# A fused attention and MLP block on one core: attention in units of two head pairs from the third query block on, with TensorE's order written out

## The chip, the core and the metric

The kernel runs on one core of a Trainium2 chip. The engines are TensorE (PE in the rows; PEld is its weight load), VectorE (DVE), ScalarE (ACT), GpSimd (POOL) and SyncE (SP), which issues the DMAs. Each works through its own queue in order, and semaphores hold an instruction until what it needs is there. The metric is the time of one execution on the device in microseconds (us), as a median over runs.

## The reference

Three stages follow each other on 2 batches of 768 tokens:

```python
# 1. attention, 8 heads of 64, a causal window of 96 keys and 8 global keys, a bias by distance
scores = scale * q @ k.T - slope[h] * dist          # only where keep
a = softmax(scores); x = a @ v                      # x: 2 x 768 x 512
# 2. channel mix
xn = (x - mean) / sqrt(var + 1e-6) * g_ln
x = x + relu(xn @ w_ch1) @ w_ch2                    # 512 -> 2048 -> 512
# 3. token mix
theta = x @ w_theta; zr, zi = x * cos(theta), x * sin(theta)
u = x + w_tok_r @ zr + w_tok_i @ zi
out = u + relu(u @ w_ch)
```

## The kernel before

**Attention** runs over 12 blocks of 128 queries (2 batches of 6). SEQ is their order, and CHUNKS groups them in twos: `[[0, 6], [1, 2], [3, 4], [5, 7], [8, 9], [10, 11]]`. The first two blocks (0 and 6, the first of each batch) see 128 keys, all others 256. A block has four head pairs p. For each pair:
- `scores` (L190): two f32 matmuls s, one for each head, on the two halves of TensorE's rows. DVE adds the bias and takes the minimum of the negated scores ("maxima", tile e, accumulator nm), ACT takes exp in place.
- `flip_probs` (L220), called flip below: TensorE transposes e into the PSUM bank pt, ACT or DVE copies it to pts.
- `values` (L235): f32 matmuls of pts with the block's v (vc) and its window's v (vw) into xa.

Per block, `finish_x` (L251) copies xa to xs on ACT, transposes it back on TensorE (xp), and DVE scales it into x2. `layer_norm` (L269) gives xn; six of the twelve blocks take two POOL operations for it (LN_DVE = 6), the others one of DVE. `make_xt` (L356) transposes xn (xnp) and splits it into xth + xtl, since a matmul in f32 precision is made of three in float32r: high x high, high x low, low x high.

**The channel mix** goes in items (c, f): chunk c of 256 tokens, f one of 16 slices of 128 hidden channels. `mlp_h` (L367) runs 12 matmuls hp, then ACT's hh (Relu) and DVE's hl; `mlp_o` (L389) runs 6 matmuls op, three for each of the chunk's two blocks, accumulated in PSUM over a group of f and then added to x2 by DVE (`add_mix`, L386). A round is 24 items: all six chunks with four f. The weights come as 58 pieces of 512 KB (raw, three buffers), each decoded to f32 by one ACT operation and three of DVE (pieces 0 to 15), and split into high and low parts by `split_w` (L338).

**The order.** A framework schedules the instructions of each engine by its own estimate and fixes one order for each. `attention` (L744) is a generator whose step n issues the scores of pair n, the flip of pair n - 2, the values of pair n - 3, and finish_x, layer_norm and make_xt at lags 6, 7 and 8. The main loop (L809) calls `steps_to` so that a chunk's xt is issued before its first item. In the first round the four f are taken in two groups of two (`beside`, L805), so that items start after two decoded pairs of pieces. TensorE's order in the attention part is thus the scheduler's: an item's matmuls are put between those of pairs one or two at a time.

`spin` (L71) issues dummy matmuls that keep TensorE busy while it would wait. PSUM has eight banks: h 2, o 2, s 2, pt 1, m 1 (L66); xp of the later blocks uses pt too.

Of the kernel before, what the change touches and what calls it, by code (L numbers as in the profile page):

```python
# [29 lines left out]
EDGE = 248  # L30
PAD = 32
# [3 lines left out]
def kernel(ctx, tc, q, kwin, v, n_pair, g_ln, wall, out):  # L35
# [12 lines left out]
    HALF = GROUP // 2  # L48
    GROUPS = [range(0, HALF), range(HALF, GROUP), *(range(f, f + GROUP) for f in range(GROUP, NF, GROUP))]
# [70 lines left out]
    maxima = []  # L120

    def behind_maximum(n):
        return tc.issue_after(maxima[n]) if n is not None else ExitStack()

# [65 lines left out]
    def scores(b, i, p, startup):  # L190
        nk = WIN if i else P
        b0 = 0 if i else WIN
        if p == 0:
            stat[b, i] = (
                at.tile([P, H], F32, tag="nm", name=f"nm{b}_{i}", bufs=2),
                at.tile([P, H], F32, tag="sm", name=f"sm{b}_{i}", bufs=2),
            )
        nm, sm = stat[b, i]
        qb, kb = qt[b, i], kt[b, i]
        s = [ps("h" if startup and p % 2 else "s", [P, nk], f"s{b}_{i}_{p}_{j}") for j in range(2)]  # L200
        k0 = WIN - nk
        for j in range(2):
            rows = slice(j * D, (j + 1) * D)
            nc.tensor.matmul(s[j], qb[rows, p, :], kb[rows, p, k0:WIN], start=True, stop=True)  # L204
        if startup:
            spin("o", f"spin{b}_{p}", 2)
        e = at.tile([P, 2, nk], F32, tag="p", name=f"e{b}_{i}_{p}", bufs=3)
# [7 lines left out]
        for j in range(2):  # L215
            h = 2 * p + j
            nc.scalar.activation(e[:, j, :], e[:, j, :], AF.Exp, bias=nm[:, h:h + 1], scale=-1.0, accum_out=sm[:, h:h + 1])  # L217
        e_t[b, i, p] = e

    def flip_probs(b, i, p, startup):  # L220
# [7 lines left out]
        pts = at.tile([P, 2, nb, P], F32, tag="pt", name=f"pts{b}_{i}_{p}", bufs=2)  # L228
        if p % 3:
            nc.scalar.activation(pts, pt, AF.Copy)  # L230
        else:
            nc.vector.tensor_copy(pts, pt)
        pts_t[b, i, p] = pts

    def values(b, i, p):  # L235
# [31 lines left out]
    LN_DVE = 6  # L267

    def layer_norm(t, at=at, gbc=gbc):  # L269
# [7 lines left out]
        if SEQ.index(t) < LN_DVE:  # L277
# [61 lines left out]
    def split_w(f):  # L339
        decode_to(2 * f + 2)  # L340
        r = []
        for d, nm in enumerate(("w1", "w2")):
# [6 lines left out]
        split_t[f] = r  # L349
# [5 lines left out]
    def make_xt(t):  # L355
# [6 lines left out]
        transposed(xn_t.pop(t), hi[:, :, sl], lo[:, :, sl], "m", f"xnp{t}")  # L362
# [3 lines left out]
    def mlp_h(c, f, tag):  # L366
# [377 lines left out]
    def attention():  # L744

        N = NTT * NPAIR

        def block(n):
            return blocks[n // NPAIR]

        def startup(n):
            return n // NPAIR < len(CHUNKS[0])

        for n in range(N + 20):
            t, p = divmod(n, NPAIR)
            if n < N:
                if p == 0:
                    loads_to(t + 2)
                scores(*blocks[t], p, startup(n))
            if 0 <= n - 2 < N:  # L760
                flip_probs(*block(n - 2), (n - 2) % NPAIR, startup(n - 2))
            if 0 <= n - 3 < N:
                values(*block(n - 3), (n - 3) % NPAIR)
            for lag, fn in ((6, finish_x), (7, layer_norm), (8, make_xt)):
                k_ = n - lag
                if k_ % NPAIR == 0 and 0 <= k_ < N:
                    tt = SEQ[k_ // NPAIR]
                    if fn is finish_x:
                        finish_x(*divmod(tt, NQ), startup(k_))
                    else:  # L770
                        fn(tt)
            yield

# [9 lines left out]
    st = attention()  # L783

    def steps_to(n):
        while n_step[0] < n:
            next(st, None)
            n_step[0] += 1

    def done_at(c):  # L790
        return NPAIR * (SEQ.index(CHUNKS[c][-1]) + 1) + 7

    spin("m", "spin", 12)
    steps_to(2)
# [10 lines left out]
    beside = [(0, 0), (0, 1), (1, 0)] + [x for c in range(2, NCH) for x in ((0, c), (1, c - 1))] + [(1, NCH - 1)]  # L805
    rest = [(g, c) for g in range(2, len(GROUPS)) for c in range(NCH)]
    work = [(g, c, f) for g, c in beside + rest for f in GROUPS[g]]
# [120 lines left out]
```

## Time and profile before

| | us |
|---|---|
| median of 3 runs | 569.44 |
| lowest, highest | 568.22, 569.63 |
| the profiled execution | 569.5 |
| its span, first to last instruction | 567.6 |
| busy: TensorE, DVE, ACT, POOL | 554.1, 366.5, 282.4, 121.8 |
| mean granted TensorE clock, share of full speed | 0.997 |

TensorE's matmuls are pipelined and a record lasts longer than the distance to the next start, so its busy time says little; the distances between starts say what a matmul costs. Records of one kind that follow each other are merged into one row of the timeline (x4 is four records).

### The profile page before, as it was taken

To read this page: it belongs to the slowest core of one execution; us is meant where nothing else is said; L and a number is where in the kernel's file an instruction comes from. 1 tells how busy PE (TensorE), PEld (TensorE's weight loads), DVE (VectorE), ACT (ScalarE), POOL (GpSimd) and SP (SyncE) were. 2 spreads that over 40 slices of the span, in tenths; PEclk is the share of its full clock that TensorE was granted. 3 is DMA by queue.
4 is the path that set the end of the run, shared out by engine and by line. 5 is a ranking of instruction groups with operands and counts; after the bars stand their busy time and mean duration, and the time that the engine had idled before them with its cause. 6 is when DMAs were issued, how large, how long until landed. Compare 5 with 4: busy or idle time off the path is not lost.

```text
span 567.6 us, 9282 instructions
## 1 busy us (share of the span) xinstructions
PE 554.1 (98%) x3532; PEld 461.9 (81%) x3532; DVE 366.5 (65%) x789; ACT 282.4 (50%) x647; POOL 121.8 (21%) x103
## 2 busy tenths in 40 slices
PE   8899999999999999999999999999999999999996
PEld 4466677777798899999999888889888888888895
DVE  6899989757458732278784524463699888871542
ACT  5887764645226511166662415561587777740110
POOL 1455420000012000030300202231033347730000
PEclk9999999999999999999999999999999999999998
DMA  8965655500003410025452000000243200000122
GB/s 271 324 214 177 218 191 205 167 1 2 0 1 112 152 34 1 1 84 208 156 186 74 1 1 1 1 2 0 75 147 120 106 1 1 1 1 1 76 74 80
DMA packets 18548, 49.18 MB, mean 87 GB/s; under 512 B 2240, under 2 KB 4288, under 8 KB 18496
## 3 DMA queue, kind: packets, MB, share of 16 engines
q1 hardware_dynamic: 18496, 48.51, 24.7%
q8 instruction: 30, 0.49, 0.4%
q14 instruction: 22, 0.18, 0.1%
HBM read 45.35 MB, written 3.15 MB: 85 GB/s over the span
## 4 chain that ended last, share of the span: by engine, by line
PE 64%; ACT 1%; DVE 1%; issue 0%; DVEq 0%; ACTq 0%
PE op L398 17%; PE acc L551 17%; PE hp L375 17%; PE thm L486 6%; PE ch L597 6%; PE xp L290 1%; ACT wt L320 0%; ACT xth L291 0%; DVE hl L380 0%; DVE w2l L347 0%; DVE x2all L387 0%; ACT w L320 0%; ACT k L494 0%; ACT k L493 0%; ACT s L499 0%
## 5 line engine op out<-in xcount | busy, mean ns | idle before, releaser
L375 PE MATMUL hp<-xth,w1h 128*128 128x256 f32 x384 | 109.0, 284 | 0.0
L375 PE MATMUL hp<-xth,w1l 128*128 128x256 f32 x384 | 108.7, 283 | 0.0
L375 PE MATMUL hp<-xtl,w1h 128*128 128x256 f32 x384 | 108.4, 282 | 0.0
L380 DVE SCALAR_TENSOR_TENSOR hl<-hp,hh 128x256 fp32r<-128x256 f32 x96 | 40.2, 420 | 79.7 <-ACT hh L379 79.4
L379 ACT ACTIVATE hh<-hp 128x256 fp32r<-128x256 f32 x96 | 36.0, 376 | 95.9 <-PE hp L375 95.9
L551 PE MATMUL acc<-tokh,z 128*128 128x512 f32 (+1 forms) x320 | 79.2, 336 | 0.0
L398 PE MATMUL op<-w2h,hh 128*128 128x512 f32 x192 | 76.9, 401 | 0.7 <-ACT hh L379 0.5
L375 PEld LDWEIGHTS hp<-xth,w1h 128*128 128x128 f32 x384 | 72.6, 189 | 6.2 <-issue 1.5
L375 PEld LDWEIGHTS hp<-xtl,w1h 128*128 128x128 f32 x384 | 72.6, 189 | 5.9 <-issue 1.7
L398 PE MATMUL op<-w2l,hh 128*128 128x512 f32 x192 | 76.1, 397 | 0.0
L398 PE MATMUL op<-w2h,hl 128*128 128x512 f32 x192 | 76.0, 396 | 0.0
L375 PEld LDWEIGHTS hp<-xth,w1l 128*128 128x128 f32 x384 | 72.6, 189 | 1.7 <-issue 1.5
L551 PEld LDWEIGHTS acc<-tokh,z 128*128 128x128 f32 x320 | 55.4, 190 | 6.5
L217 ACT ACTIVATE e<-e,nm 128x256 f32<-128x256 f32 (+1 forms) x96 | 46.2, 482 | 26.8 <-DVE nm L210 24.8
L551 PE MATMUL acc<-tokl,z 128*128 128x512 f32 (+1 forms) x160 | 53.8, 336 | 0.0
L347 POOL TENSOR_TENSOR w1l<-w,w1h 128x512 fp32r<-128x512 f32 x16 | 22.3, 1391 | 136.1 <-ACT w1h L346 136.1
L387 DVE SCALAR_TENSOR_TENSOR x2all<-op,rsall,x2all 128x512 f32<-128x512 f32 x60 | 42.8, 743 | 6.8 <-PE op L398 6.8
L513 POOL TENSOR_TENSOR x2all<-xth,xtl 128x512 f32<-128x512 f32 x12 | 18.3, 1524 | 121.2 <-DVE k L505 121.2
L398 PEld LDWEIGHTS op<-w2h,hl 128*128 128x128 f32 x192 | 36.1, 188 | 8.9 <-DVE hl L380 0.2
L210 DVE CUSTOM_DVE_ANT_0 e<-s,bias 128x256 f32<-128x256 f32 (+1 forms) x96 | 35.4, 392 | 11.4 <-PE s L204 10.6
L398 PEld LDWEIGHTS op<-w2h,hh 128*128 128x128 f32 x192 | 36.4, 190 | 5.7 <-ACT hh L379 0.7
L463 DVE TENSOR_TENSOR tokl<-wt,tokh 128x512 fp32r<-128x512 f32 x36 | 33.9, 950 | 10.3 <-ACT tokh L462 10.1
(155 smaller groups left out, 1074.1 us busy)
## 6 DMA issues: line engine op xcount, KB each, us to landing
raw<-in_wall SPq DMA_DIRECT2D x58, 512.0 KB, 3.2
k<-in_kwin SPq DMA_DIRECT2D x10, 512.0 KB, 5.7
q<-in_q SPq DMA_DIRECT2D x12, 256.0 KB, 4.0
vc<-in_v SPq DMA_DIRECT2D x12, 256.0 KB, 3.2
out<-o SPq DMA_DIRECT2D x8, 256.0 KB, 2.0
vw<-in_v SPq DMA_DIRECT2D x10, 192.0 KB, 2.7
out<-o SPq DMA_DIRECT2D x8, 128.0 KB, 2.2
vw<-in_v SPq DMA_DIRECT2D x10, 64.0 KB, 3.7
```

The lines of the kernel that those rows point to most:

```text
L210: r = nc.vector.tensor_tensor_reduce(out=e[:, j, :], in0=s[j], in1=bias[h][:, b0:b0 + nk], scale=-SCALE, scalar=3.0e38, op0=ALU.add, op1=A ...
L217: nc.scalar.activation(e[:, j, :], e[:, j, :], AF.Exp, bias=nm[:, h:h + 1], scale=-1.0, accum_out=sm[:, h:h + 1])
L347: (nc.vector if d and f >= GROUP else nc.gpsimd).tensor_tensor(lo, s, hi.bitcast(F32), ALU.subtract)
L375: nc.tensor.matmul(hp, l, r[:, kk, :], start=(n == 0), stop=(n == 3 * KD - 1))
L379: nc.scalar.activation(hh, hp, AF.Relu)
L380: nc.vector.scalar_tensor_tensor(hl, hp, 0.0, hh.bitcast(F32), ALU.max, ALU.subtract)
L387: nc.vector.scalar_tensor_tensor(x2[t], o, rsall[:, t:t + 1], x2[t], ALU.mult, ALU.add)
L398: nc.tensor.matmul(op_t[c][j], l, r, start=(f == fs[0] and n == 0), stop=(f == fs[-1] and n == 2))
L463: nc.vector.tensor_tensor(lo, src, hi.bitcast(F32), ALU.subtract)
L486: nc.tensor.matmul(mp, l[:, kk, :], r[:, kk, :], start=(n == 0), stop=(n == 3 * KD - 1))
L551: mm = nc.tensor.matmul(o, l[:, dsl], r[:, sl], start=first and not (paired and d % 2), stop=end and not (paired and d % 2 == 0))
L597: nc.tensor.matmul(mp, l[:, kk, es], r, start=(kk == 0 and m == 0), stop=(kk == KD - 1 and m == 2))
```

## The change

The first two blocks keep their order, left to the scheduler (`head_step`). From the third block on a loop over k issues, on TensorE alone in exactly the order of the code (`tc.manual_schedule`), one unit (two head pairs of a block: scores, later two flips and two values) and one item of the first round. hp of an item is cut in two halves of six matmuls with a flip between them, op in two halves by block, xp and xnp go between those. In steps 0 to 5 one piece each is decoded and split (pieces 2 to 7) and from step 7 on one piece per two steps (decoded only). The first three steps have no mix and fill up with five dummy matmuls at a time. The first round takes its four f in one group, so 48 adds replace 60. In the first two blocks' flips and in all others, ACT copies pairs 0 and 2 and DVE 1 and 3 (before: ACT 1 and 2). xs is copied right behind a block's values (`lift_x`); xnp moves from bank m to a bank h; xn is DVE's for all blocks (LN_DVE = 0); e gets a fourth buffer; a unit's scores of one head side share one bank.

```diff
-    GROUPS = [range(0, HALF), range(HALF, GROUP), *(range(f, f + GROUP) for f in range(GROUP, NF, GROUP))]
+    GROUPS = [range(f, f + GROUP) for f in range(0, NF, GROUP)]
...
+    def scores(b, i, ps_, startup):
...
+        n = len(ps_)
+        s = [ps("h" if startup and ps_[0] % 2 else "s", [P, n, nk], f"s{b}_{i}_{ps_[0]}_{j}") for j in range(2)]
+        k0 = WIN - nk
+        for a, p in enumerate(ps_):
+            for j in range(2):
+                rows = slice(j * D, (j + 1) * D)
+                nc.tensor.matmul(s[j][:, a, :], qb[rows, p, :], kb[rows, p, k0:WIN], start=True, stop=True)
...
-        if p % 3:
+        if p % 2 == 0:
             nc.scalar.activation(pts, pt, AF.Copy)
...
-    LN_DVE = 6
+    LN_DVE = 0
...
-        transposed(xn_t.pop(t), hi[:, :, sl], lo[:, :, sl], "m", f"xnp{t}")
+        transposed(xn_t.pop(t), hi[:, :, sl], lo[:, :, sl], "h", f"xnp{t}")
...
+    U = 2
+    NU = (NTT - HEAD) * U
+    LEAD = 3
+    items = [(c, f) for c in range(NCH) for f in GROUPS[0]]
...
+    with tc.manual_schedule(engines=ENGINES):
+        for k in range(LEAD + len(items) + 1):
+            j = k - LEAD
+            u = k - 1
+            mix = 0 <= j < len(items)
+            xp_of = HEAD + (k - 3) // U if k % U == 1 and 0 <= (k - 3) // U < NTT - HEAD else None
+            xt_of = HEAD + (k - 4) // U if k % U == 0 and 0 <= (k - 4) // U < NTT - HEAD else None
...
+            if 0 <= u < NU:
+                flip_probs(*unit(u)[:2], unit(u)[2][0], False)
+            if k < NU:
+                b, i, ps_ = unit(k)
+                if k % U == 0:
+                    loads_to(HEAD + k // U + 2)
+                scores(b, i, ps_, False)
...
+            if mix:
+                mlp_h(*items[j], "h", 0)
+            elif 0 < k < LEAD:
+                spin("o", f"idle{k}", 5)
+            if 0 <= u < NU:
+                flip_probs(*unit(u)[:2], unit(u)[2][1], False)
+            if mix:
+                mlp_h(*items[j], "h", 1)
+            if xt_of is not None:
+                make_xt(SEQ[xt_of])
+            if 0 <= j - 1 < len(items):
+                down(j - 1, [0])
+            if xp_of is not None:
+                finish_x(*blocks[xp_of], False)
+            if 0 <= j - 1 < len(items):
+                down(j - 1, [1])
+            if 0 < k < LEAD:
+                spin("o", f"wait{k}", 5)
+            if 0 <= u < NU:
+                for p in unit(u)[2]:
+                    values(*unit(u)[:2], p)
+                if u % U == U - 1:
+                    lift_x(*unit(u)[:2])
+            if xp_of is not None:
+                layer_norm(SEQ[xp_of])
+            if 0 <= k < 2 * GROUP - 2:
+                with behind_exp(len(maxima) - 1):
+                    split_w((k + 2) // 2, ((k + 2) % 2,))
+            elif k >= 7:
+                with behind_maximum(min(len(maxima) - 1, 16 + 4 * k + 3)):
+                    decode_to(2 * GROUP + min(NW, (k - 5) // 2))
```

Where TensorE stood in block 0_4 and 0_5 (batch 0, blocks 4 and 5; the second number of a pair's tile is p), the order before was this:

```order
L204 MATMUL s0_5_0_0_983<-k0_5_645,q0_5_644 128x256
L204 MATMUL s0_5_0_1_984<-k0_5_645,q0_5_644 128x256
L375 MATMUL hp1_0_1180<-xth1_675,w1h0_269 128x256
L227 MATMUL pt0_4_2_992<-ident_65,e0_4_2_826 128x128 x4
L246 MATMUL xa0_4_958<-pts0_4_1_956,vw0_4_500 64x128
L246 MATMUL xa0_4_958<-pts0_4_1_956,vc0_4_498 64x128
L246 MATMUL xa0_4_958<-pts0_4_1_956,vw0_4_500 64x128
L246 MATMUL xa0_4_958<-pts0_4_1_956,vc0_4_498 64x128
L204 MATMUL s0_5_1_0_1012<-k0_5_645,q0_5_644 128x256
L204 MATMUL s0_5_1_1_1013<-k0_5_645,q0_5_644 128x256
L375 MATMUL hp1_0_1180<-xtl1_676,w1h0_269 128x256
```

and now, at the end of step 9 and the beginning of step 10 (hp of item 6 stands ahead of these rows, hp of item 7 behind), it is:

```order
L429 MATMUL op1_0_1_1133<-w2h1_540,hh1_1_1120 128x512
L429 MATMUL op1_0_1_1133<-w2l1_541,hh1_1_1120 128x512
L429 MATMUL op1_0_1_1133<-w2h1_540,hl1_1_1121 128x512
L284 MATMUL xp4_1203<-ident_65,xs0_4_1149 128x128 x4
L429 MATMUL op1_0_2_1134<-w2h1_540,hh1_1_1120 128x512
L429 MATMUL op1_0_2_1134<-w2l1_541,hh1_1_1120 128x512
L429 MATMUL op1_0_2_1134<-w2h1_540,hl1_1_1121 128x512
L264 MATMUL xa0_5_1212<-pts0_5_0_1156,vw0_5_723 64x128 x2
L264 MATMUL xa0_5_1212<-pts0_5_0_1156,vc0_5_721 64x128 x2
L264 MATMUL xa0_5_1212<-pts0_5_1_1186,vw0_5_723 64x128 x2
L264 MATMUL xa0_5_1212<-pts0_5_1_1186,vc0_5_721 64x128 x2
L245 MATMUL pt0_5_2_1237<-ident_65,e0_5_2_1164 128x128 x4
```

One hp stood between a pair's scores and the next flip, and each pair's values stood alone; now op and xp stand together, and two pairs' values behind each other. Behind the last row come the four matmuls of scores of the next unit and six hp.

On DVE the same step is, from the decode of piece 9 on (the maxima of the unit stand ahead of it):

```order
L351 TENSOR_SCALAR dec9_1233<-w9_1229 128x512
L250 COPY pts0_5_1_1186<-pt0_5_1_1181 128x512
L352 SCALAR_TENSOR_TENSOR dec9_1233<-w9_1229,dec9_1233 128x512
L410 SCALAR_TENSOR_TENSOR hl1_2_1195<-hp1_2_1174,hh1_2_1194 128x256
L285 TENSOR_TENSOR x2all_70<-xp4_1203,sm0_4_914 128x512
L353 SCALAR_TENSOR_TENSOR w9_1229<-raw9_796,dec9_1233 128x512
L297 BN_STATS bn4_1221<-x2all_70 128x6
L280 TENSOR_SCALAR sm0_5_1083<-sm0_5_1083 128x8
L298 BN_AGGR mv4_1222<-bn4_1221 128x2
L281 RECIPROCAL sm0_5_1083<-sm0_5_1083 128x8
L304 SCALAR_TENSOR_TENSOR xn4_1225<-x2all_70,mv4_1222,gbc_95 128x512
```

where the program before had, around its decode of piece 9:

```order
L328 TENSOR_SCALAR dec9_2160<-w9_2156 128x512
L210 ISA e0_5_2_1036,nm0_5_981<-s0_5_2_0_1032,bias4_102 128x256
L210 ISA nm0_5_981 128x1
L210 ISA e0_5_2_1036,nm0_5_981<-s0_5_2_1_1033,bias5_103 128x256
L210 ISA nm0_5_981 128x1
L329 SCALAR_TENSOR_TENSOR dec9_2160<-w9_2156,dec9_2160 128x512
L232 COPY pts0_5_0_1046<-pt0_5_0_1041 128x512
```

Now four maxima stand together ahead of the decode, the pts copy behind its first operation, and xn (before POOL's for this block) is DVE's.

In the beginning, behind the first two blocks, TensorE now has (steps 0 and 1; idle0 are dummy matmuls, s0_1_0 and pt0_1_0 belong to the third block):

```order
L231 MATMUL s0_1_0_0_422<-k0_1_163,q0_1_162 128x256
L231 MATMUL s0_1_0_1_423<-k0_1_163,q0_1_162 128x256
L231 MATMUL s0_1_0_0_422<-k0_1_163,q0_1_162 128x256
L231 MATMUL s0_1_0_1_423<-k0_1_163,q0_1_162 128x256
L264 MATMUL xa1_0_372<-pts1_0_2_396,vc1_0_147 64x128 x2
L264 MATMUL xa1_0_372<-pts1_0_3_403,vc1_0_147 64x128 x2
L245 MATMUL pt0_1_0_456<-ident_65,e0_1_0_428 128x128 x4
L231 MATMUL s0_1_2_0_463<-k0_1_163,q0_1_162 128x256
L231 MATMUL s0_1_2_1_464<-k0_1_163,q0_1_162 128x256
L231 MATMUL s0_1_2_0_463<-k0_1_163,q0_1_162 128x256
L231 MATMUL s0_1_2_1_464<-k0_1_163,q0_1_162 128x256
```

The scores of the second unit stand behind the first flip of the first, so behind its exp; before, the scheduler had put scores of three pairs ahead of the third block's first flip.

## Rows read from the trace of the kernel before

**Rows 1.** Windows: PE, PEld, DVE, ACT, POOL busy (instructions), clock, DMA share, GB/s.

```profile
16.00:61.00 45.00, 41.44 (x310) 26.93 (x312) 42.34 (x128) 36.44 (x111) 23.46 (x19) 1.00 0.68 232
61.00:149.00 88.00, 85.68 (x648) 63.45 (x647) 69.67 (x207) 47.83 (x141) 11.51 (x12) 1.00 0.34 115
```

**Rows 2.** The chain that ended last, by time: start us, us, what.

```profile
189.28 1.64 PE op L398 x6
...
193.79 1.40 PE op L398 x6
195.19 1.42 PE hp L375 x12
```

**Rows 3.** Groups of TensorE, 60.81 to 149.11 us: records, busy us, mean ns, idle before.

```profile
L204 PE MATMUL s<-k,q 64*128 64x256 f32 x96 | 17.2, 428 | 0.0
...
L375 PE MATMUL hp<-xth,w1h 128*128 128x256 f32 x48 | 14.1, 294 | 0.0
...
L398 PE MATMUL op<-w2h,hl 128*128 128x512 f32 x25 | 10.0, 398 | 0.0
...
L290 PE MATMUL xnp<-ident,xn 128*128 128x128 f32 x24 | 3.9, 284 | 1.6 <-ACT xs L256 1.6
```

**Rows 4.** TensorE's waits, 61 to 149 us: total us, times, longest.

```profile
PE xnp L290 <- ACT xs L256: 1.6, 3, 0.8
```

**Rows 5.** TensorE's timeline from 61.45 us: start us, us, records.

```profile
61.45 0.66 PE L227 MATMUL pt<-ident,e 128*128 128x128 f32 x4
62.03 0.45 PE L246 MATMUL xa<-pts,vw 128*64 128x128 f32 x4
...
62.63 0.70 PE L204 MATMUL s<-k,q 64*128 64x256 f32 x4
63.26 0.39 PE L375 MATMUL hp<-xth,w1h 128*128 128x256 f32 x1
63.70 0.65 PE L227 MATMUL pt<-ident,e 128*128 128x128 f32 x4
```

**Rows 6.** TensorE's timeline in the first two blocks, scores of 128 keys.

```profile
5.67 0.49 PE L204 MATMUL s<-k,q 64*128 64x128 f32 x4
6.10 0.61 PE L75 MATMUL spin<-zero 128*128 128x512 bf16 x2
...
12.46 0.71 PE L204 MATMUL s<-k,q 64*128 64x128 f32 x8
13.11 0.44 PE L227 MATMUL pt<-ident,e 128*128 128x128 f32 x2
```

**Rows 7.** TensorE's timeline from 58.17 us: transposes, half an hp, op.

```profile
58.17 0.60 PE L261 MATMUL xp<-ident,xs 128*128 128x128 f32 x4
58.52 0.36 PE L375 MATMUL hp<-xth,w1h 128*128 128x256 f32 x1
...
59.32 0.40 PE L398 MATMUL op<-w2h,hh 128*128 128x512 f32 x1
```

**Rows 8.** TensorE's timeline from 30.27 us: two pairs' values in a row.

```profile
30.27 0.45 PE L246 MATMUL xa<-pts,vw 128*64 128x128 f32 x4
...
31.35 1.35 PE L204 MATMUL s<-k,q 64*128 64x256 f32 x4
```

**Rows 9.** DVE's timeline: the last operation on piece 3.

```profile
35.86 0.68 DVE L330 SCALAR_TENSOR_TENSOR w<-raw,dec 128x512 int32<-128x512 int32 x1
```

**Rows 10.** Groups by shape, 0 to 189 us: exp, maxima, add, pts, xn.

```profile
L217 ACT ACTIVATE e<-e,nm 128x256 f32<-128x256 f32 x80 | 39.9, 500 | 20.8 <-DVE nm L210 18.8 <-DVE mv L275 1.8
L210 DVE CUSTOM_DVE_ANT_0 e<-s,bias 128x256 f32<-128x256 f32 x80 | 31.4, 413 | 9.4 <-PE s L204 9.3
...
L387 DVE SCALAR_TENSOR_TENSOR x2all<-op,rsall,x2all 128x512 f32<-128x512 f32 x23 | 16.5, 743 | 3.3 <-PE op L398 3.3
...
L232 DVE COPY pts<-pt 128x512 f32<-128x512 f32 x20 | 13.7, 686 | 2.7 <-PE pt L227 2.3
...
L281 DVE SCALAR_TENSOR_TENSOR xn<-x2all,mv,gbc 128x512 f32<-128x512 f32 x6 | 4.5, 747 | 0.1
```

More of the change, by code (lines that the diff above doesn't have):

```diff
@@ L188, with soften @@
     n_step = [0]
-    def scores(b, i, p, startup):
-        nk = WIN if i else P
+    def soften(b, i, p, e, s):
+        nk = e.shape[-1]
         b0 = 0 if i else WIN
[L193 to L197, printed above, removed]
-        nm, sm = stat[b, i]
[L199 to L207, printed above, removed]
+        nm, sm = stat[b, i]
         for j in range(2):
@@ L742, in loads_to @@
             nloaded[0] += 1
[L744 to L772, printed above, removed]
     words = keep.tile([P, 2, 2], I32, name="words")
@@ L782, with behind, head_step @@
     loads_to(1)
[L783 to L791, printed above, removed]
+    HEAD = len(CHUNKS[0])
+    ROWS = range(NPAIR)
+    def behind(n):
+        return divmod(n, NPAIR)
+    def head_step(n):
+        t, p = divmod(n, NPAIR)
+        if t < HEAD:
+            if p == 0:
+                loads_to(t + 2)
+            scores(*blocks[t], [p], True)
+        for lag, fn in ((2, lambda b, i, p: flip_probs(b, i, p, True)), (3, values)):
+            if 0 <= n - lag < HEAD * NPAIR:
+                t, p = divmod(n - lag, NPAIR)
+                fn(*blocks[t], p)
+                if lag == 3 and p == NPAIR - 1:
+                    lift_x(*blocks[t])
+                    finish_x(*blocks[t], True)
     spin("m", "spin", 12)
-    steps_to(2)
+    for n in range(2):
+        head_step(n)
     next(bias_steps)
@@ L806, with unit, down @@
-    rest = [(g, c) for g in range(2, len(GROUPS)) for c in range(NCH)]
-    work = [(g, c, f) for g, c in beside + rest for f in GROUPS[g]]
-    early, done = iter(()), [0]
+    U = 2
+    NU = (NTT - HEAD) * U
+    LEAD = 3
+    items = [(c, f) for c in range(NCH) for f in GROUPS[0]]
+    def unit(k):
+        t, h_ = divmod(k, U)
+        return (*blocks[HEAD + t], [2 * h_, 2 * h_ + 1])
+    def down(j, js):
+        c, f = items[j]
+        mlp_o(c, f, GROUPS[0], js)
+        if js[-1] and c == NCH - 1 and f + GROUP < NF:
+            split_w(f + GROUP)
@@ L809 @@
+    work = [(g, c, f) for g in range(len(GROUPS)) for c in range(NCH) for f in GROUPS[g]]
+    early, done = iter(()), [ROUND]
     for n, (g, c, f) in enumerate(work):
+        if n < ROUND:
+            continue
         rnd = n // ROUND
         if n == ROUND:
-            steps_to(NTT * NPAIR + 20)
             at_es.close()
```

116 lines of the change are left out of this document (81 added, 35 removed).

## The prediction

> **What bounds the kernel now.** I read the windows first, to see which engine is full where. From 16 to 61 us DVE is busy 42.34 of 45 us; from 61 to 149 us TensorE is busy 85.68 of 88 [rows 1]. [...] The chain that ended last is TensorE's from 189.28 us on: op and hp of the channel mix, one behind the other, at 1.40 and 1.42 us, 2.82 an item [rows 2]. So what the attention part saves before that point comes off the end, if nothing new is late at the border. What stays after it (72 items, then the token mix) is not touched.
>
> A busy TensorE is not a TensorE at its peak, so I counted what it gets done. Between 60.81 and 149.11 us, 88.30 us, it runs 96 score records, 96 transposes of probabilities, 192 value records, 144 records of hp, 73 of op, 24 of xnp and 24 of xp [rows 3] (four of these groups stand there; hp and op have three forms each). An f32 matmul leaves two records, a transpose one. That is 24 head pairs, 12 items (12 hp, 6 op each) and six blocks' xp and xnp: 12 steps of the changed program, at 88.30 / 12 = **7.36 us a step**. Little of it is waiting: the longest of TensorE's waits in 61 to 149 us, xnp's, sum to 1.6 us [rows 4].
>
> The rest is the price of changing over. The timeline shows it in start times [rows 5]: four transposes 61.45 to 62.03 = 0.58, a pair's values 62.03 to 62.63 = 0.59, a pair's scores 62.63 to 63.26 = 0.63, and then a single hp 63.26 to 63.70 = 0.44. In a stream of its own kind that hp costs 1.42 / 12 = 0.118. An item takes 2.82 when it runs whole, and before 149 us it seldom does.
>
> **The change on TensorE, step by step.** The new order is flip, two pairs' scores, six hp, flip, six hp, three op, three op, two pairs' values, with xnp (even steps) or xp (odd steps) among them.
> - Flip after values: 0.58 [rows 5].
> - Two pairs' scores. No row has them with 256 keys. With 128 keys one pair takes 5.67 to 6.10 = 0.42 and two in a row 12.46 to 13.11 = 0.65 [rows 6]: the second adds 0.23. With 256 keys it adds at least that and at most a pair's whole 0.63. I take 0.43, between the two, since a record streams twice the columns while the start and the drain are paid once: **1.06**.
> - Six hp: 6 x 0.118 = 0.71. Four transposes inside a stream cost 0.355 (58.17 to 58.52), and six hp after them 0.80 instead of 0.71 (58.52 to 59.32) [rows 7]. So flip 0.355, hp 0.80, xnp or xp 0.355.
> - Six op: 1.40, and by the same rows 0.09 behind a transpose, and 0.10 for the change to values: 1.59.
> - Two pairs' values: the trace has them once, 30.27 to 31.35 = 1.08 [rows 8], against 2 x 0.59.
>
> Sum: 0.58 + 1.06 + 0.71 + 0.355 + 0.80 + 0.355 + 1.59 + 1.08 = **6.53 us**, 0.83 less than 7.36.
>
> [...]
>
> **The beginning.** The first two blocks run much as before. Steps k = 0, 1, 2 have no mix, and DVE sets their pace: it decodes pieces 0 to 3 around them (three operations each), and each unit's maxima stand behind those. The old DVE ended piece 3 at 36.5 [rows 9]. By the order, DVE has until the end of unit 2's maxima two maxima (0.41) and two pts copies (0.69) less to do than the old one until then, and two xn (0.75) more, which were POOL's [rows 10]: 36.5 - 2.2 + 1.5 = 35.8 at the same pace. Behind it stand the pts copy of unit 1, 0.69, and its values on TensorE, 1.08, so step 3, the first with a mix, starts at 37.6. I take **38**. Bounds: 35, if DVE loses the 2.7 us that it was idle in 16 to 61 us [rows 1]; 44, if in each of the three steps it waits 2 us for scores behind flips that wait for exp. The 25 new dummy matmuls (two last 0.61 [rows 6], so five some 1.4) lie under these waits; without that cover they cost 7.
>
> **The sum.** Step 3 has no op: 5.1. Steps 4 to 19: 16 x 6.53 = 104.5. Step 20 has no scores: 5.4. Step 21 is an item and xp: 3.3; step 22 an item and xnp: 3.3, plus 0.4, since x2, bn and xn (three times 0.7 on DVE) stand between xp and that xnp. Steps 23 to 26: 4 x 2.82 = 11.3. Step 27: 1.4. End of the 24 items: 38 + 5.1 + 104.5 + 5.4 + 3.3 + 3.7 + 11.3 + 1.4 = 172.7. The old program starts the op of item 24 at 189.28 with the hp of items 24 and 25 behind it, so its 24 items end at 189.28 - 2 x 1.42 = 186.4. The gain is 13.7. I take 1 us off for two places where a queue may hold: ACT's first operations on pieces 8 and 9 stand before a pts copy in step 6, and SP issues piece 9 behind loads that wait for a block's values. So 12.7. The profiled execution took 569.5 (span 567.6, 1.9 around it), the median is 569.44: 569.5 - 12.7 = **557**.
>
> **What costs nothing, and its cover.** DVE in two steady steps: 8 maxima x 0.413, ten operations of 128x512 (two pts, three of a decode, x2, xtl, bn, xn, and one add on average) at some 0.70, two hl and the small ones at some 1.6 together: 11.9 us by the means of [rows 10], less in truth, as one record begins before the last ends. Two steps of TensorE are 13.06. So xn of six blocks moved to DVE (6 x 0.75) is hidden, and the 12 adds removed (one accumulation over four f instead of two over two; 12 x 0.74 = 8.9) bring nothing by themselves; were a step shorter than 5.9, both would count in full. Inside an odd step, DVE can begin its four maxima 1.4 us after the start (the first pair's scores are out) and ends them, one decode operation and the pts copy some 2.4 later, at 3.8; xp wants that bank at 4.3. In the step that also has two adds DVE runs 1.5 us into the next; that one's maxima then end at 3.6, the four exp (0.50 each) by 6.0, and their flip comes at 6.5. Both margins are half a microsecond.
>
> **The rivals.**
> 1. *The written order waits on DVE in each step* (slower). What stands behind a late xp or flip on TensorE, the rest of the item, waits with it, and the margins are thin. xnp waits already now, up to 0.8 [rows 4]. Should every step from 3 to 19 wait 1.2 us, the time is 557 + 20 = 577. It decides from 0.9 a step on (15 us over 17 steps). Against it: 11.9 of 13.06 on DVE, and ACT busy 47.83 of 88 us [rows 1].
> 2. *Scores in twos save nothing*: 17 steps x 0.2 = 3.4 more, 560. [...]
> 3. *The beginning eats it*: step 3 at 50 instead of 38 gives 569, no change. For it speaks that scores of two pairs now wait for the maxima of the two before; against it, that DVE is full there in both programs with as much to do.
> 4. *More than forecast*: a second pair at 0.23 (-3.4) and the beginning at 35 (-3) give 550.
>
> **Chances.** Forecast 0.70 (551 to 566); rival 2 0.08; rival 4 0.08; rival 1 0.08; rival 3 0.03, and 0.03 for a gain of which only 2 to 3 us are left. 0.3% (1.7 us) is about what a measurement of this kernel can tell: faster 0.89, same 0.03, slower 0.08. The bounds (beginning -3 to +6, scores -3.4 to +3.4, waits up to +8) don't fall together; 551 to 566 holds eight in ten.
>
> **What would show it.** Right: a step of 6.4 to 6.7 us, from one first flip to the next, in 65 to 140 us, eight score records lasting 1.0 to 1.1 to the next start, the first op at about 47 us instead of 59.32, DVE idle for a tenth or more there, and the chain TensorE's alone from about 175. [...]

## The result, and the profile after

The changed kernel takes 563.26 us (median of 4 runs, 562.99 to 563.6), the kernel before 568.89 us beside it: a ratio of 0.990, 95% interval 0.988 to 0.992. It is faster by 5.6 us, or 1%; 12.7 us were forecast. The time lies inside the stated range of 551 to 566 us, but the gain is less than half of the forecast one. The profiled span is 561.4 us, 6.2 less than before.

Three windows of the changed kernel, the columns as in [rows 1]: the beginning, the steady steps, and what follows the last scores.

```profile
16.00:40.00 24.00, 19.76 (x146) 11.82 (x145) 20.12 (x58) 16.94 (x53) 6.58 (x6) 1.00 0.70 243
60.00:150.00 90.00, 90.00 (x736) 72.33 (x735) 68.49 (x221) 53.16 (x161) 5.11 (x8) 1.00 0.32 107
150.00:180.00 30.00, 27.43 (x186) 22.62 (x186) 20.54 (x39) 13.64 (x27) 6.97 (x6) 1.00 0.22 73
```

From 60 to 150 us the trace lists no wait of TensorE any more; before 60 and behind 150 it lists some. One steady step in TensorE's timeline, from a unit's first flip to the next unit's:

```profile
65.81 0.66 PE L245 MATMUL pt<-ident,e 128*128 128x128 f32 x4
66.40 1.14 PE L231 MATMUL s<-k,q 64*128 64x256 f32 x8
67.46 0.39 PE L403 MATMUL hp<-xth,w1h 128*128 128x256 f32 x1
...
68.27 0.60 PE L245 MATMUL pt<-ident,e 128*128 128x128 f32 x4
68.63 0.36 PE L403 MATMUL hp<-xth,w1h 128*128 128x256 f32 x1
...
69.42 0.40 PE L429 MATMUL op<-w2h,hh 128*128 128x512 f32 x1
...
71.34 0.44 PE L264 MATMUL xa<-pts,vw 128*64 128x128 f32 x4
...
72.37 0.44 PE L245 MATMUL pt<-ident,e 128*128 128x128 f32 x2
```

72.37 - 65.81 = 6.56 us, against 7.36 before; scores of two pairs 67.46 - 66.40 = 1.06. The middle of the forecast holds. What doesn't hold is the two ends, as the starts of the steps show. A step starts at its first flip, and from step 21 on, where there are no flips, at its first hp:

| part | forecast, us | measured, us | late by |
|---|---|---|---|
| step 3 starts | 38 | 39.89 | 1.9 |
| step 3 | 5.1 | 46.03 - 39.89 = 6.14 | 1.0 |
| steps 4 to 19 | 104.5 | 151.17 - 46.03 = 105.14 | 0.6 |
| step 20 | 5.4 | 157.68 - 151.17 = 6.51 | 1.1 |
| steps 21, 22 | 7.0 | 164.94 - 157.68 = 7.26 | 0.3 |
| steps 23 to 27 | 12.7 | 179.98 - 164.94 = 15.04 | 2.3 |

Together that is 179.98 - 172.7 = 7.3 us: the 24 items end at 179.98 instead of 172.7, which is still 6.4 earlier than the old 186.4. Nearly all of it reaches the end (6.2 us of the span).

TensorE's waits in the changed kernel, 16 to 45 us (total us, times, longest):

```profile
PE xa L264 <- DVE pts L250: 1.5, 2, 1.1
PE pt L245 <- ACT e L212: 1.4, 2, 0.8
PE pt L245 <- ACT pts L248: 1.2, 1, 1.2
```

Step 3 has two short ones, for DVE's copy of the probabilities and for DVE's x2:

```profile
43.95 0.66 PE L284 MATMUL xp<-ident,xs 128*128 128x128 f32 x4 [0.28 <-DVE pts L250]
...
46.03 0.63 PE L245 MATMUL pt<-ident,e 128*128 128x128 f32 x4 [0.40 <-DVE x2all L285]
```

The waits from 145 to 190 us:

```profile
PE op L429 <- DVE hl L410: 1.4, 2, 1.1
PE xnp L313 <- DVE rsall L305: 0.7, 1, 0.7
PE xnp L313 <- DVE xn L304: 0.4, 1, 0.4
```

The waits for xnp are in steps 20 and 22. The waits for hl are at the border, that is in the last items of the first round, steps 23 to 27. ACT, DVE, POOL and TensorE there:

```profile
172.62 0.62 ACT L370 ACTIVATE w2h<-w 128x512 fp32r<-128x512 f32 x1
173.14 0.66 ACT L347 ACTIVATE dec<-raw 128x512 int32<-128x512 uint32 x1
173.71 0.62 ACT L370 ACTIVATE w1h<-w 128x512 fp32r<-128x512 f32 x1
173.88 0.69 DVE L348 SCALAR_TENSOR_TENSOR dec<-w,dec 128x512 int32<-128x512 int32 x1
174.23 0.36 ACT L409 ACTIVATE hh<-hp 128x256 fp32r<-128x256 f32 x1
174.45 1.29 POOL L371 TENSOR_TENSOR w1l<-w,w1h 128x512 fp32r<-128x512 f32 x1 [2.43 <-ACT w1h L370]
...
174.66 1.63 DVE L349 SCALAR_TENSOR_TENSOR w<-raw,dec 128x512 int32<-128x512 int32 x1
...
176.22 0.41 DVE L410 SCALAR_TENSOR_TENSOR hl<-hp,hh 128x256 fp32r<-128x256 f32 x1
...
176.68 0.50 PE L429 MATMUL op<-w2h,hl 128*128 128x512 f32 x1 [1.08 <-DVE hl L410]
```

The hp of the item whose hh and hl stand in these rows had ended at some 172.2. Its hh comes 2 us later, behind a decode and two splits in ACT's queue. Its hl starts 1.6 us after hh has ended, behind a decode operation in DVE's queue that takes 1.63 us instead of 0.69. The chain that ended last runs through that operation and DVE's next ones until 178.95, and not through TensorE:

```profile
174.66 1.63 DVE w L349
176.29 0.34 DVE hl L410
...
178.95 1.20 PE op L429 x4
```

In the beginning DVE is idle for 3.9 of 24 us. Its timeline there:

```profile
20.11 1.45 DVE L352 SCALAR_TENSOR_TENSOR dec<-w,dec 128x512 int32<-128x512 int32 x1
...
23.43 1.09 DVE L280 TENSOR_SCALAR sm<-sm 128x8 f32<-128x8 f32 x1
...
28.38 0.43 DVE L351 TENSOR_SCALAR dec<-w 128x512 int32<-128x512 int32 x1 [1.69 <-ACT w L343]
...
35.61 0.68 DVE L353 SCALAR_TENSOR_TENSOR w<-raw,dec 128x512 int32<-128x512 int32 x1
...
37.90 0.69 DVE L250 COPY pts<-pt 128x512 f32<-128x512 f32 x1
```

The last decode ahead of step 3, the maxima behind it and this pts copy come 1.8 us after the forecast 35.8 for the maxima's end (37.59). Ahead of that DVE waits 1.69 us for ACT's first operation on piece 2, and two of its operations take longer, 1.45 instead of 0.69 us (the second of piece 1's decode) and 1.09 instead of 0.17 (sm).

### The profile page after: what moved, and what is told of

It is laid out like the page before. It is cut to its first block, busy times and chain, and to the rows that moved or that the text cites. A ratio compares the mean times of both kernels' runs of the same rounds, so it can differ in the third digit from the quotient of the medians.

```text
span 561.4 us, 9278 instructions
## 1 busy us (share of the span) xinstructions
PE 546.8 (97%) x3554; PEld 461.9 (82%) x3557; DVE 359.8 (64%) x783; ACT 280.6 (50%) x647; POOL 103.4 (18%) x91
## 4 chain that ended last, share of the span: by engine, by line
PE 66%; ACT 1%; DVE 1%; issue 0%; DVEq 0%; ACTq 0%
PE op L429 18%; PE hp L403 18%; PE acc L582 17%; PE thm L517 6%; PE ch L628 6%; PE xp L313 1%; DVE w L349 0%; ACT wt L343 0%; DVE hl L410 0%; ACT xth L314 0%; DVE dec L348 0%; ACT k L525 0%; ACT k L524 0%; ACT s L530 0%; ACT y L523 0%
## 5 line engine op out<-in xcount | busy, mean ns | idle before, releaser
L403 PE MATMUL hp<-xth,w1h 128*128 128x256 f32 x384 | 111.3, 290 | 0.0
L429 PE MATMUL op<-w2h,hh 128*128 128x512 f32 x192 | 78.5, 409 | 0.0
L409 ACT ACTIVATE hh<-hp 128x256 fp32r<-128x256 f32 x96 | 35.8, 374 | 74.4 <-PE hp L403 74.4
L205 DVE CUSTOM_DVE_ANT_0 e<-s,bias 128x256 f32<-128x256 f32 (+1 forms) x96 | 33.5, 397 | 16.8 <-PE s L231 16.7
L429 PEld LDWEIGHTS op<-w2l,hh 128*128 128x128 f32 x192 | 36.2, 188 | 3.8
```

Of the source, the lines that this page charges most:

```text
L205: r = nc.vector.tensor_tensor_reduce(out=e[:, j, :], in0=s[j], in1=bias[h][:, b0:b0 + nk], scale=-SCALE, scalar=3.0e38, op0=ALU.add, op1=A ...
L409: nc.scalar.activation(hh, hp, AF.Relu)
L429: nc.tensor.matmul(op_t[c][j], l, r, start=(f == fs[0] and n == 0), stop=(f == fs[-1] and n == 2))
```

## The experiments

**The changed kernel again**, as a base on one chip for the second group of runs.

> The changed kernel itself, unedited, so that the kernels beside it are compared with it on one chip: the ratio of 0.990 to the kernel before is expected again, and steps 23 to 27 at 15.0 us. It also says how far one profile of the same kernel differs from another in the start of step 3 (39.9 before).

0.9903 (0.9887 to 0.9919), 563.91 us; step 3 starts at 40.36, steps 23 to 27 take 15.03. So a start can differ by 0.5 between two profiles of one kernel, a step's length by 0.05. Most of the 0.5 lies ahead of the first scores, which start at 6.06 and at 6.42: counted from there, step 3 starts after 33.83 and 33.94 us. Where the ratios below are weighed, this run is the base.

**Decode held at the border.**

```diff
+        relus.append((r.ins, r2.ins))
...
-        decode_to(2 * GROUP * (rnd + 1) + min(NW, n % ROUND // 2))
+        with tc.issue_after(relus[ROUND - 1][0]), tc.issue_after(relus[ROUND - 1][1]):
+            decode_to(2 * GROUP * (rnd + 1) + min(NW, n % ROUND // 2))
```

> Pieces 16 and up are decoded only behind the relu operations of the 24th item on ACT and DVE; nothing else is moved. Theory A (at the border the decode of pieces 16 to 18, two operations of 0.67 us on ACT and two of 0.69 us on DVE each, stands ahead of hh and hl of items 22 and 23): steps 23 to 27 shrink from 15.05 us to about 13.0, the 24 items end near 178.0 instead of 179.98, and the time falls by about 2 us, to 561.3. [...] Theory C (the decode is then late in the second round): the border shrinks, but the total does not.

0.9855 (0.9835 to 0.9876), 561.84 us. The timeline of ACT, DVE and POOL with the decode held:

```profile
175.22 0.63 ACT L370 ACTIVATE w1h<-w 128x512 fp32r<-128x512 f32 x1 [0.67 <-PE hp L404]
175.76 0.36 ACT L410 ACTIVATE hh<-hp 128x256 fp32r<-128x256 f32 x1
175.99 1.30 POOL L371 TENSOR_TENSOR w1l<-w,w1h 128x512 fp32r<-128x512 f32 x1 [1.52 <-ACT w1h L370]
176.03 0.67 ACT L343 ACTIVATE w<-raw 128x512 f32<-128x512 f32 x1
176.16 0.42 DVE L411 SCALAR_TENSOR_TENSOR hl<-hp,hh 128x256 fp32r<-128x256 f32 x1 [0.88 <-ACT hh L410]
```

The splits are there as before, but hh now stands ahead of the decode, hl follows it at once, and TensorE waits for neither: steps 23 to 27 take 177.95 - 165.11 = 12.84 us, near the 12.7 of the forecast. That is theory A. The ratio falls by as much and more (0.9903 to 0.9855, some 2.7 us), so nothing is seen to be paid back later.

**xnp behind half of op in steps 20 and 22.**

```diff
-            if xt_of is not None:
+            if xt_of is not None and k < NU:
                 make_xt(SEQ[xt_of])
             if 0 <= j - 1 < len(items):
                 down(j - 1, [0])
+            if xt_of is not None and k >= NU:
+                make_xt(SEQ[xt_of])
```

> In steps 20 and 22, which have no scores, xnp stands behind the first half of op instead of ahead of it. Theory A (xnp waits there for xn and rsall, 1.0 and 0.66 us, because a step without scores is shorter than DVE's way from xp over x2, bn and xn): step 20 shrinks from 6.51 to about 5.6 us, step 22 from 3.88 to 3.4 to 3.9, and the time falls by 1.0 to 1.4 us, to 562. Theory B (the wait only moves, to hp of the item that reads the block, or DVE's queue is late for all that follows): steps 20 to 22 together keep their 13.8 us and the time stays within 0.4 us of 563.3.

0.9893 (0.9875 to 0.9911), not to be told from the base. Step 20 takes 5.82 instead of 6.51 us, step 22 3.42 instead of 3.88, but the twelve hp behind it last 2.14 instead of 1.57: they wait for that block's xth and xtl. Up to the end of these hp 0.6 us are saved. It is theory A for step 20 and theory B for step 22.

**Both at the border**: the hold, and the later xnp in step 20 alone.

```diff
+            if xt_of is not None and k == NU:
+                make_xt(SEQ[xt_of])
```

> Two edits at the border together: pieces 16 and up are held behind the relu operations of the 24th item (as in the first of these runs, which took some 2.3 us off), and in step 20 alone xnp stands behind the first half of op (step 22 as in the changed kernel, since its wait only moved). Theory A (the two losses lie one behind the other on TensorE and add up): steps 20 to 22 take 13.1 instead of 13.8 us, steps 23 to 27 12.7, and the time is 3.0 us under the changed kernel, 560.5 to 561, a ratio of 0.985. Theory B (the later xnp makes ACT and DVE late at the border again): no more than the 2.3 us of the hold alone.

0.9835 (0.9807 to 0.9862), 561.7 us, the fastest of the kernels that leave nothing out. Steps 20 to 22 take 164.54 - 151.49 = 13.05 us, steps 23 to 27 12.84. By the steps this is theory A: 0.7 + 2.2 of the lost 7.3 us are explained and got back. By the time alone it can't be told from the hold alone (0.9855).

**No dummies.**

```diff
-                spin("o", "idle0", 5)
...
-            elif 0 < k < LEAD:
-                spin("o", f"idle{k}", 5)
...
-            if 0 < k < LEAD:
-                spin("o", f"wait{k}", 5)
```

> The 25 dummy matmuls of steps 0 to 2 are left out. Theory A (they lie under waits, as forecast): step 3 starts at 39.9 less the one stretch that has no wait behind it, idle0 at 22.6 to 23.8, so between 38.8 and 39.9, and the time is 562.2 to 563.3. [...] Theory C (they cost what they last): step 3 starts 3 us earlier or more, and the time is 560 or less.

0.9914 (0.9894 to 0.9934), 565.02 us; step 3 starts at 40.50 and lasts 7.01. Windows of this kernel, the columns as in [rows 1]:

```profile
24.00:28.00 4.00, 2.08 (x18) 1.17 (x14) 2.65 (x12) 3.06 (x10) 0.97 (x2) 1.00 0.71 254
28.00:32.00 4.00, 2.23 (x22) 1.71 (x20) 3.81 (x13) 3.65 (x12) 0.75 (x1) 1.00 0.66 213
32.00:36.00 4.00, 2.95 (x16) 2.21 (x18) 3.98 (x10) 1.31 (x4) 1.06 (x2) 0.60 0.29 115
36.00:40.00 4.00, 4.00 (x24) 2.74 (x24) 2.27 (x10) 2.91 (x10) 1.67 (x2) 0.55 0.36 131
```

In this profile TensorE is busy for 4.31 of the 8 us from 24 to 32, then the granted clock is 0.60 and 0.55 in 32 to 40 us (1.00 in the changed kernel), and the scores of unit 2 take 2.01 instead of 1.16 us. The waits for pts, 1.5 us in all with the dummies, are 4.0 without. But the time shows no loss from it: the ratio can't be told from the base's 0.9903, and the start of step 3, counted from the first scores, is 34.52, 0.6 to 0.7 later. The earlier starts of theories A and C did not come. So the dummies cost nothing that these runs show, and what they save is not shown to reach the time.

**Scores of unit 0 early.**

```diff
             if k == 0:
+                loads_to(HEAD + 2)
+                scores(*unit(0), False)
                 flip_probs(*blocks[1], 2, True)
...
-            if k < NU:
+            if 0 < k < NU:
```

> In the beginning the scores of unit 0 (two pairs of the third block) stand ahead of the last flips and values of the second block, instead of behind them and the dummies. Theory A (in 16 to 40 us DVE idles for 3.9 us because its maxima of unit 0 come only at 25.3, after TensorE's written order let the scores run at 23.8): the maxima begin at 20 to 22, step 3 starts at 37.5 to 38.5 instead of 39.9, step 3 no longer waits for pts, and the time falls by 1.5 to 2.5 us, to 561 to 562. Theory B (DVE has that much to do in any order): step 3 starts at 39.4 or later and the time stays within 0.5 us of 563.3.

0.9882 (0.9863 to 0.9902), not to be told from the base. The first pair's scores run at 15.4, the second's at 17.1, but step 3 starts at 39.61: 0.3 and 0.75 earlier than in the two profiles of the changed kernel, or some 0.4 counted from the first scores (33.48). Step 3 takes 5.78 instead of 6.13. That is less than half of theory A.

**Decode not held in steps 0 to 5.**

```diff
-                with behind_exp(len(maxima) - 1):
-                    split_w((k + 2) // 2, ((k + 2) % 2,))
+                split_w((k + 2) // 2, ((k + 2) % 2,))
```

> In steps 0 to 5 the six pieces that are decoded and split there are no longer held behind the maxima and exp of the newest unit; the scheduler puts them where it finds room. Theory A (DVE idles at 26.6 to 28.4 us because the first operation of piece 2 on ACT is held behind the exp of unit 0, and this is half of the 1.9 us by which step 3 starts late): that idle stretch is filled, step 3 starts at 38.0 to 39.0 and the time falls by 1 to 2 us. Theory B (decoding ahead only puts the same work ahead of the maxima and exp for which the flips wait): step 3 starts at 39.9 or later, TensorE's waits for e and pts before 45 us grow above 5 us, and the time is the same or up to 2 us more.

0.9976 (0.9962 to 0.9991), 567.4 us. TensorE's waits, 16 to 195 us:

```profile
PE xp L284 <- DVE pts L250: 2.5, 1, 2.5
PE xa L264 <- DVE pts L250: 2.3, 3, 1.2
```

DVE is now busy for 27.64 of 29 us between 16 and 45 instead of 24.43, and it is worse: step 3 starts at 41.78 and takes 9.33 us. Theory B: filling DVE's idle time puts the decode ahead of the copies for which TensorE waits. It costs more than the 2 us that theory B allowed: by the ratio some 4 us over the base.

**Pieces later.** Pieces 2 to 7 one step later (the edit below), then piece 1 too, which leaves the first two blocks for step 0:

```diff
-            if 0 <= k < 2 * GROUP - 2:
+            if 1 <= k < 2 * GROUP - 1:
                 with behind_exp(len(maxima) - 1):
-                    split_w((k + 2) // 2, ((k + 2) % 2,))
+                    split_w((k + 1) // 2, ((k + 1) % 2,))
```

> Pieces 2 to 7 are decoded and split one step later each (steps 1 to 6 instead of 0 to 5), held behind the newest exp as before. Theory A (DVE sets the pace of steps 0 to 2; a piece fewer ahead of step 3 saves its three operations, 1.7 us, there, and the steps behind have room for it): step 3 starts 1.0 to 1.7 us earlier, at 38.2 to 39.3, no later step waits for a weight, and the time falls by 1 to 2 us. Theory B (the way from scores over maxima, exp, flip, copy to values sets the pace of steps 0 to 2 whatever DVE does beside): step 3 starts within 0.4 us of 39.9 to 40.4, and the time stays. Theory C (the piece is missed in steps 4 to 7): step 3 is earlier, but hp or op of items 1 to 3 waits for w1l, w2l, and the time is the same or more.

> As the run beside it, and piece 1 too leaves the first two blocks for step 0, so that step 0 has piece 1, step 1 piece 2 and so on. [...] Theory B: as there.

0.9902 (0.9873 to 0.9931) and 0.991 (0.988 to 0.994): nothing. Step 3 starts at 39.72 and 39.11. Counted from the first scores that is 33.29 and 32.70, so some 0.6 and 1.2 us are won of 1.7 and 3.4 taken from DVE's queue; then step 6 takes 8.40 us in both, where hp waits 0.7 us for w1h and 0.8 for w1l of the fourth weight. By the theories of the first of the two it is C for the total, and too little won for A.

**Pieces later, none missed**, with the border edits; then two dummies for five:

```diff
-                    split_w((k + 2) // 2, ((k + 2) % 2,))
+                for x in {4: (5, 6), 5: (7,)}.get(k, (k + 1,)):
...
+                        split_w(x // 2, (x % 2,))
```

> Both border edits, and pieces 1 to 7 later: 1 to 4 in steps 0 to 3, 5 and 6 in step 4, 7 in step 5, so that the w1 half of the fourth weight is no longer missed in step 6, which cost 1.85 us in the two runs before. Theory A (pieces ahead of step 3 cost about a third of their DVE time there, 1.25 us for two pieces, and nothing later once none is missed): step 3 starts at 38.9 to 39.3, step 6 takes 6.6, and the time is 1.2 us under that of the border edits alone, a ratio of 0.981 to 0.982 to the kernel before, some 559.5 us. Theory B (two pieces in step 4 make flips or xp wait there): step 4 or 5 takes a microsecond more, and the ratio stays at 0.9835.

```diff
-                spin("o", f"idle{k}", 5)
+                spin("o", f"idle{k}", 2)
...
-                spin("o", f"wait{k}", 5)
+                spin("o", f"wait{k}", 2)
```

> As the run beside it, with two dummy matmuls instead of five at each of the four places in steps 1 and 2. [...] Theory B (DVE's copy for the values ends last in step 2 anyway): the waits for pts take up what the dummies leave, step 3 starts at 38.7 or later, and the time stays. [...]

0.9891 (0.9864 to 0.9918) and 0.9893 (0.9865 to 0.992): 3 us slower than with the border edits alone. In the first, step 3 starts at 38.85, but step 5 takes 9.21 us and step 6 8.37: in step 5 xp waits 2.4 us for pts, behind the decode of two pieces (theory B). In the second, step 2 takes 4.97 instead of 5.95 us and step 3 hands it back (7.27 instead of 6.13): steps 1 to 3 take 19.82 us with two dummies and 19.67 with five, theory B. Step 5 is as long (9.18), step 6 is 6.58; why step 6 is shorter was not looked into. The starts of these two can't be compared. In the second's profile the granted clock is 0.87, 0.50 and 0.78 in 16 to 20, 20 to 24 and 24 to 28 us (0.88 over 16 to 45), 1.00 in the first's, though TensorE's order up to the scores of unit 0 is the same; the scores of unit 0 come 19.5 instead of 16.9 us after the first scores. So the time says nothing certain about the dummies.

**No decode on DVE at all** for pieces 0 to 7, with five and with two dummies:

```diff
+    first_order, skipped = order, {}
...
+        if i < 2 * GROUP and order is first_order and not skipped.get(i):
+            skipped[i] = True
+            return
         t = rawp.tile([P, DM], I32, tag="dec", name=f"dec{i}", bufs=1)
```

> The changed kernel with DVE's three operations left out of the decode of pieces 0 to 7 (the weights then lack their lower bits, so the output is another); ACT's copies, the splits and the written order stay. This takes 5 x 1.7 us of DVE's queue away ahead of step 3 and another 5 us in steps 3 to 6. Theory A (DVE's amount of work sets the beginning): step 3 starts before 36 and lasts 5.1 us, steps 4 to 6 have no wait. Theory B (TensorE's own written order with its dummies, and the way from scores to values, set it): step 3 starts at 38.0 to 39.2, and only step 3's own wait goes away. Between them, what is left of the 1.9 us is TensorE's.

> As the run beside it, with two dummy matmuls instead of five at each of the four places in steps 1 and 2. [...]

One run each, 562.54 and 559.75 us beside 569.43 for the kernel before. First flips of steps 2, 3 and 4 with five dummies:

```profile
34.02 0.66 PE L245 MATMUL pt<-ident,e 128*128 128x128 f32 x4
...
39.88 0.66 PE L245 MATMUL pt<-ident,e 128*128 128x128 f32 x4
...
45.65 0.63 PE L245 MATMUL pt<-ident,e 128*128 128x128 f32 x4 [0.22 <-DVE x2all L285]
```

The same with two:

```profile
32.55 0.66 PE L245 MATMUL pt<-ident,e 128*128 128x128 f32 x4
...
37.20 0.66 PE L245 MATMUL pt<-ident,e 128*128 128x128 f32 x4
...
42.98 0.63 PE L245 MATMUL pt<-ident,e 128*128 128x128 f32 x4 [0.22 <-DVE x2all L285]
```

With five, step 2 still takes 5.86 us (5.94 with the decode): flip, scores, xnp, ten dummies, flip and values one behind the other, no wait among them. With two it takes 4.65. Step 3 takes 5.77 and 5.78, not 5.1, with no decode in its way. In both runs the granted clock fell to 0.63 and 0.72 in 20 to 24 us, and the scores of unit 0 come 18.5 and 18.6 us after the first scores instead of 17.7, so neither start of step 3 can be held against the changed kernel's. From the scores of unit 0 to step 3 it is 16.1 us in the changed kernel, 15.2 without the decode, 12.8 with two dummies as well. It is theory B for step 2, and theory A's 36 is not reached. Between these two runs step 3 moves by 2.7 us (39.88 to 37.20), so TensorE's own order with its dummies sets steps 1 and 2 there.

**One pair at a time.**

```diff
-                scores(b, i, ps_, False)
+                late = scores(b, i, ps_, False)
...
+            if k < NU:
+                late()
             if 0 <= u < NU:
                 flip_probs(*unit(u)[:2], unit(u)[2][1], False)
...
+            if 0 <= u < NU:
+                values(*unit(u)[:2], unit(u)[2][0])
             if 0 <= j - 1 < len(items):
                 down(j - 1, [1])
```

> The written order is kept, but the two pairs of a unit no longer run back to back: the second pair's scores stand behind the first six hp, the first pair's values between the two halves of op. Nothing is added or left out. Theory A (the gain is the price of changing over that pairing saves): scores cost 2 x 0.63 instead of 1.06, values 2 x 0.59 instead of 1.03, the flip behind scores and the op behind values some 0.1 each, so a step takes 7.0 to 7.2 us instead of 6.56, seventeen steps 8 to 11 us more, and the time is 571 to 574, slower than the kernel before. Theory B (the gain comes from the order being written at all, or from the adds that fell away): a step stays under 6.75 and the time under 566.

1.0232 (1.0214 to 1.025), 583.0 us: slower than before. TensorE's timeline of an undelayed step, first flip, scores, scores, next first flip:

```profile
89.33 0.66 PE L261 MATMUL pt<-ident,e 128*128 128x128 f32 x4
89.91 0.70 PE L237 MATMUL s<-k,q 64*128 64x256 f32 x4
...
91.45 0.72 PE L237 MATMUL s<-k,q 64*128 64x256 f32 x4
...
96.61 0.33 PE L261 MATMUL pt<-ident,e 128*128 128x128 f32 x1
```

A step takes 96.61 - 89.33 = 7.28 us, 0.73 more than paired and nearly the old 7.36: theory A, if a little over its 7.0 to 7.2. The matmuls inside a pair's values also stand in another order than before (one vw and one vc in turn before, two and two now). That is not the gain: a pair's values alone take 0.59 us here, as in the kernel before. The rest of the 19 us I had not expected: five times the second pair's scores wait for DVE's maxima (2.3 us listed; those five steps take 8.0 to 8.3, together 4.6 us more than five others), and step 3 starts 3.3 us later.

**One more operation on DVE in each step.**

```diff
-            elif k >= 7:
+            if 4 <= k < NU:
+                with behind_maximum(len(maxima) - 1):
+                    nc.vector.tensor_tensor(junk, gbc, gbc, ALU.add)
+            if k >= 7:
```

> In each of steps 4 to 19 DVE gets one more operation on 128x512 (about 0.6 us of its queue), behind the unit's maxima, whose output nobody reads. Theory A (the cover is as thin as the prediction's sum had it, 11.9 of 13.06 us on DVE in two steps, margins of half a microsecond): two more operations of 0.6 use the 1.16 up, flips or xp begin to wait, steps take 6.6 to 7.0 us and the time rises by 1 to 7 us. Theory B (the trace's own count, DVE busy for 68.5 of 90 us between 60 and 150, means 3 us of room in two steps): the steps stay at 6.56 and the time within 0.7 us of the changed kernel's.

0.9958 (0.9944 to 0.9972), 567.06 us, 3.1 more. Steps 4 to 19 take 153.82 - 46.26 = 107.56 us, 2.45 more than in the base, for 16 operations of 0.6. DVE is busy for 73.83 of 90 us, and yet steps get longer, as theory A has it: odd ones by 0.22, step 5 by 0.9, even ones not at all. So in the odd steps 0.6 us more costs 0.22, which leaves a margin of some 0.4 us, near the half microsecond of the prediction; in the even steps the margin is at least 0.6. The prediction's sum for DVE was too high (11.9 us in two steps; the trace has 68.49 / 90 x 13.1 = 10.0).

## Why the prediction was half right

**The steady step** was right: 6.56 against 6.53 us, scores 1.06, both flips, the second six hp and op to 0.02. The first six hp take 0.81 instead of 0.71 behind the scores, two pairs' values 1.03 instead of 1.08. The 1.06 was a choice between two bounds, and that it came out to the hundredth is luck. That pairing is the gain is shown: undone in the same written order, the step is 7.28. Rival 2 fell: two pairs' scores take 1.06 us and not 2 x 0.63 = 1.26, so the second pair adds 0.43 and not the 0.63 of a pair alone. Why it costs less, no run shows; nor does one show the start and the drain, which the prediction took as paid once, by themselves. Rival 1 fell as well, with thin margins.

**The step that failed is "The sum"**, in the terms for its two ends: what TensorE waits for there was put at nothing or too little.

- *Steps 23 to 27* (12.7, measured 15.04). I priced the four last items by TensorE alone. "If nothing new is late at the border" stood as a condition, but had no price; the chain was to be TensorE's alone from about 175 us, and it is DVE's until 178.95. It was not the splits of the next weights by themselves: with the decode of pieces 16 and up held, they stand as close and steps 23 to 27 take 12.84. They may have a part in it: beside a split on POOL (174.45 to 175.74) the decode operation on DVE takes 1.63 instead of 0.69 us; what the decode would cost without that was not tried. That decode's place on ACT and DVE is left to the scheduler, whose order could have been read at the border as I read it at the units.
- *Step 20* (5.4, measured 6.51) and *step 3* (5.1, measured 6.14). I got both by taking a full step and subtracting what they lack on TensorE. What TensorE waits for in them doesn't shrink with it: in step 20 x2, bn and xn stand between xp and xnp, which I had priced for step 22 only (xnp waits 0.7 us; with xnp later the step is 5.82). In step 3 xp waits 0.28 us for DVE's pts copy, and the next flip 0.40 for x2; it takes 5.77 even with DVE's decode gone, where the wait for x2 is still 0.22.
- *The beginning* (38, measured 39.9). Of the 1.9 us, 0.4 lie ahead of the first scores (6.06, 5.67 in the profile of the old kernel [rows 6]), where the profiles of this study scatter from 5.67 to 6.43; that share is no part of the change that any run shows. "DVE sets their pace" was half of the rest. DVE was idle for 3.9 of 24 us, where the old one was for 2.7 of 45 [rows 1]; "at the same pace" was the wrong assumption. And "the 25 new dummy matmuls lie under these waits" is true only while the waits are there (five take 1.18 us to the next start, not 1.4): in step 2 the trace lists no wait of TensorE, and ten of them stand in its order. In step 2 the two bounds lie within 0.1 us of each other: without the decode it takes 5.86 instead of 5.94 us, and with fewer dummies as well 1.3 us less. But the decode has to be done somewhere: with two dummies and the decode step 3 hands the microsecond back, and with the pieces later steps 5 and 6, or step 6 alone, get longer.

*The 1 us off for two queue holds* was not needed: step 6 took 6.55. *Rival 3* (the beginning eats the gain) had the right place and a quarter of the size (2.9 of 12 us). The rest of what the beginning loses is not settled piece by piece: which share of the 1.9 us is DVE's wait for ACT's operation and which the two longer operations was not tried alone, and that cause stays open.

## What to carry to other kernels

Price the ends of a written order like its middle, by what TensorE waits for there: a step that lacks work on the bound engine is as long as the way beside it, not as the work left. Where a scheduler keeps placing the other engines' work, read its order at every place where the change brings work closer together, and hold back what has time; holding the decode back at the border gave 2.2 us. Work that hides under a wait is free only until the wait goes, so ask what bounds next before taking anything out of a queue.

## What the runs showed of the hardware

- Some operations of DVE took longer while one of POOL ran. DVE's operation at 174.66 takes 1.63 instead of 0.69 us: POOL's w1l ends at 174.45 + 1.29 = 175.74, and 0.55 later DVE's ends. The two longer ones in the beginning, at 20.11 (1.45 instead of 0.69) and 23.43 (only 8 columns, 1.09 instead of 0.17), end 0.55 and 0.03 us behind POOL's operations:

```profile
19.74 1.27 POOL L371 TENSOR_TENSOR w1l<-w,w1h 128x512 fp32r<-128x512 f32 x1 [17.64 <-ACT w1h L370]
23.23 1.26 POOL L371 TENSOR_TENSOR w2l<-w,w2h 128x512 fp32r<-128x512 f32 x1 [2.22 <-ACT w2h L370]
```

  Others did not: beside POOL's w1l from 31.59 to 32.87 DVE's x2 at 32.02 takes 0.68, as the six from 71 to 137 us do, where none of POOL's splits runs, and with the decode held at the border hl at 176.16 takes 0.42 beside w1l from 175.99 to 177.29 (0.42 is its mean in the changed kernel). One of POOL's took longer too: w1l at 170.18 lasts 1.85 and the one before it, at 167.36, 1.30; a DVE operation of 0.69 began together with it. What makes the difference, no run shows.
- TensorE's granted clock fell in some profiles and not in others. Without the 25 dummy matmuls it is 0.60 and 0.55 in 32 to 40 us, behind 8 us in which TensorE was busy for 4.31; with them it is 1.00 there in both profiles of the changed kernel. In the two runs without the decode TensorE is busy for 2.24 of the 4 us from 16 to 20, and the clock is 0.63 and 0.72 in 20 to 24; in the changed kernel it is busy for 2.76, and the clock is 1.00. But of the two runs with the pieces later and none missed, whose order is the same up to the scores of unit 0, the second is at 0.50 in 20 to 24 us (0.88 over 16 to 45) and the first stays at 1.00. In the second the scores of unit 0 come 2.6 us later, but the two median times are alike (564.0 and 564.06 us). So the dummies are not shown to hold the clock in every execution.
